# Attention in one written order of single operations, small matmuls between single dense matmuls

## The chip, the cores and the metric

The kernel runs on 1 core of one Trainium2 chip. The metric is device time in microseconds (us), the median of 3 runs. Inside the core five engines work at once, each on a queue of its own that it takes strictly in the order in which the program was compiled: TensorE (PE, matmuls; the loading of a matmul's stationary operand is shown apart, as PEld), VectorE (DVE), ScalarE (ACT), GpSimd (POOL) and SyncE (SP, which here issues DMAs). Instructions wait for each other over semaphores.

## The reference

A pre-norm block over 2048 tokens of width 1024: attention with a compressive memory, then a channel MLP. What matters here, cut down:

```
D, H, Dh, N, L = 1024, 32, 32, 4, 512          # four segments of 512 tokens
y = layernorm(x);  q, k, v = y @ wq, y @ wk, y @ wv          # per head: 512 x 32 a segment
for s in range(N):
    p = softmax(q_s k_s^T * Dh**-0.5 + causal mask)          # 512 x 512
    a_dot = p @ v_s
    a_mem = (phi(q_s) @ M) / (phi(q_s) @ z + 1e-6)           # phi(t) = t+1 if t > 0 else exp(t)
    out_s = g * a_mem + (1 - g) * a_dot                      # g = sigmoid(beta), per head
    M += phi(k_s)^T @ v_s;  z += sum(phi(k_s))
h = x + concat(out) @ wo
h2 = h + (gelu(layernorm(layernorm(h)) @ w1 + b1) @ w2 + b2)
```

## The kernel before, in words

All products are done in a reduced fp32 form on pairs: a number is split into a high and a low part (`kh`, `kl`), and one product takes three matmuls (high by high, high by low, low by high), all added up in one PSUM tile.

The program does two halves of 1024 tokens, each with two segments: segments 0 and 1 in the first half, 2 and 3 in the second. In a half, attention goes through 8 groups `g` of four heads and two segments `sl`, so through 16 units. A unit has two sides that run at the same time, the second one unit late:

- **The dense side** (`dense`): three projections of the unit's group, `kps`, `qps`, `vps`, each 8 chunks of 3 matmuls of 128x512, so 72 single dense matmuls. From each projection follow copies and splits on ACT and DVE (`kh`, `kl`, `qh`, `ql`, `vt`), the feature maps (`e`, `r` and their sum), and 12 DMAs on SP that stack the parts of `k` into the tiles `ks`, and 12 for `qs`.
- **The heads of the unit before** (`heads`, `slot`): for each of four heads, the scores `pqk` (4 matmuls of 128 to 512 columns, function `qk`), the negated scaled maximum on DVE (`mx`), the exponential on ACT, the normalising on POOL (`norm`), 10 transposes of 128x128 into `ppt` (`ptr`), their high part on ACT (`pth`) and low part on DVE (`ptl`), and 8 matmuls into `po` (`av`), then the output on ACT and DVE (`ot`). A head is spread over three slots: scores in one, transposes in the next, `po` in the one after.
- **Small matmuls** of 128 columns: 4 transposes each of `pk` (into `pkn`), `vt` (into `vn`) and `om` (into `pom`), 12 matmuls into `pm` (reading the memory, segments 1 to 3) and 12 into `pmm` (its update, segments 0 to 2). A unit has up to 36 of these, a unit of segment 3 has 20, one of segment 0 has 20. `pm` is read by four DVE operations (`memory`), `pmm` by five (`update`: four adds into `MZ` and one more).

PSUM has three buffers (tag `d`) for all of the projections, `pkn`, `vn`, `pm`, `pmm` and `pom`, two for `pqk`, two for `ppt`, one for `po`.

What sets the order around the change: `PLAN` is six steps a slot, and one step is taken after each chunk of three dense matmuls; `one_small` puts a small matmul ahead of a transpose or between two `po` matmuls; `late` holds the second part of a unit's small work. In the attention part the program's order is then a proposal: the framework's scheduler may place an instruction earlier or later on its engine by its own planned times. Only where the code uses `in_order` (the opening, the parts after attention) is the written order binding. The last unit's heads run beside the first matmuls of the output projection (`wo_first`, tiles `pwo`), and during the last dense unit seven loads `orr` bring outputs back from DRAM, which ACT copies into `oh` and DVE or POOL splits (`load_o`).

Of the kernel before, what the change touches and what calls it, by code (L numbers as in the profile page):

```python
# [9 lines left out]
F32 = mybir.dt.float32  # L10
# [6 lines left out]
P = 128  # L17
# [11 lines left out]
RA, RH, RS, PD, PS = 1.3, 14, 0.7, 20, 3  # L29
PLAN = ('q1 S2', 'q0 n0 a0', 'q2 t0 a1', 'q3 n2 s0 o', 't1', 's1 t2')  # L30
# [12 lines left out]
def build(tc, x, wq, wk, wv, wo, beta, w1, b1, w2, b2, out):  # L43
# [292 lines left out]
    def attention(half, first):  # L336
# [15 lines left out]
        def phi_parts(ps):  # L352
            e, r = tmp("e"), tmp("r")
            nc.scalar.activation(e, ps, AF.Exp)
            nc.scalar.activation(r, ps, AF.Relu)
            return e, r

        def phi_sum(parts, name, acc=None):
            o = tmp(name)
            nc.vector.scalar_tensor_tensor(o, parts[0], 1.0, parts[1], op0=ALU.min, op1=ALU.add, accum_out=acc)  # L360
            return o

        def stack(a, b, name, order):
            out = []
            for j in range(4):
                st = ab.tile([96, 512], F32R, tag=name, name=name, bufs=5)
                for blk, src in enumerate(order):
                    nc.sync.dma_start(raw(st[32 * blk:32 * blk + 32, :]), raw((a, b)[src][32 * j:32 * j + 32, :]))
                out.append(st)
            return out  # L370

        small = []

        def one_small():
            if small:
                small.pop(0)()

        def smalls(name, groups, last):
# [12 lines left out]
            small.extend(partial(one, k, n) for k in range(len(groups)) for n in range(3))  # L391

        def dense(g, sl, ws, u):
            s = 2 * half + sl
            behind = acts.pop("late", iter(()))
            kps = ws.pop("kps", None)
            if kps is None:
                kps = ps_dense("kps")
                for c in project(ws["k"], sl, "kps", kps):
                    if c >= 2:  # L400
                        next(behind, None)
                    yield
            kh, kl = tmpr("kh"), tmpr("kl")
            nc.scalar.copy(kh, kps)
            if s < 3:
                kparts = phi_parts(kps)
            qps = ps_dense("qps")
            for c in project(ws["q"], sl, "qps", qps):
                if c == 0:
                    nc.vector.tensor_tensor(kl, kps, raw(kh), op=ALU.subtract)  # L410
                    u["ks"] = stack(kh, kl, "ks", (0, 1, 0))
                if c == 2 and s < 3:
                    zc = ab.tile([P, 64], F32, name="zc", bufs=2)[:, 0:1]
                    pk = phi_sum(kparts, "pk", zc)
                next(behind, None)
                yield
            qh, ql = tmpr("qh"), tmpr("ql")
            nc.scalar.copy(qh, qps)
            if s > 0:
                qparts = phi_parts(qps)  # L420

            vps = ps_dense("vps")
            for c in project(ws["v"], sl, "vps", vps):
                if c == 0:
                    nc.vector.tensor_tensor(ql, qps, raw(qh), op=ALU.subtract)
                    u["qs"] = stack(qh, ql, "qs", (0, 0, 1))
                if s > 0:
                    if c == 2:
                        pq = phi_sum(qparts, "pq")
                    if c == 4:  # L430
                        while small:
                            one_small()
                        pqh, pql = tmpr("pqh"), tmpr("pql")
                        mzh = ab.tile([P, 256], F32R, name="mzh", bufs=1)[:, 0:132]
                        mzl = ab.tile([P, 256], F32R, name="mzl", bufs=1)[:, 0:132]
                        nc.scalar.copy(pqh, pq)
                        nc.vector.tensor_copy(mzh, MZ[:, g, :])
                        nc.gpsimd.tensor_tensor(mzl, MZ[:, g, :], raw(mzh), op=ALU.subtract)
                    if c == 5:
                        nc.gpsimd.tensor_tensor(pql, pq, raw(pqh), op=ALU.subtract)  # L440
                if c == 1 and s < 3:
                    pkn = ps_dense("pkn")
                    for i in range(4):
                        nc.tensor.transpose(pkn[:, i * P:(i + 1) * P], pk[:, i * P:(i + 1) * P], ident)
                    pkh, pkl = tmpr("pkh"), tmpr("pkl")
                    nc.scalar.copy(pkh, pkn)
                if c == 2 and s < 3:
                    nc.vector.tensor_tensor(pkl, pkn, raw(pkh), op=ALU.subtract)
                next(behind, None)
                yield  # L450
# [6 lines left out]
            def late():  # L457
# [39 lines left out]
                while len(small) > total - left:  # L497
                    yield
# [899 lines left out]
```

## Time and profile before

| what | value |
|---|---|
| median of 3 runs | 2358.24 us (2356.2 to 2359.72) |
| span of the profiled execution, first to last instruction | 2354.0 us |
| TensorE clock granted, mean | 0.995 |
| PE, share of the span | 97% |
| DVE, ACT, POOL, share of the span | 67%, 52%, 45% |

Of the profiled execution the profile gives the span alone; the runs are 2.2 to 5.7 us above it.

The units with heads are the stretches from 72 to 485 us (first half) and from 968 to 1377 us (second half). In them PE is busy 97% to 99% of the time, DVE about 76%, ACT about 71%.

How to read the rows: a timeline row gives the start, the duration, the engine, the line, the operation and `out<-in`. Matmuls are pipelined and their ends are modelled, so a dense matmul is shown with 0.39 us although the next one starts 0.23 us after it. What a matmul costs PE is therefore the distance from its start to the next start, and idle time in front of a matmul can hide behind the shown duration of the one ahead.

### The profile page before, as it was taken

To read this page: it belongs to the slowest core of one execution; us is meant where nothing else is said; L and a number is where in the kernel's file an instruction comes from. 1 tells how busy PE (TensorE), PEld (TensorE's weight loads), DVE (VectorE), ACT (ScalarE), POOL (GpSimd) and SP (SyncE) were. 2 spreads that over 40 slices of the span, in tenths; PEclk is the share of its full clock that TensorE was granted. 3 is DMA by queue.
4 is the path that set the end of the run, shared out by engine and by line. 5 is a ranking of instruction groups with operands and counts; after the bars stand their busy time and mean duration, and the time that the engine had idled before them with its cause. 6 is when DMAs were issued, how large, how long until landed. Compare 5 with 4: busy or idle time off the path is not lost.

```text
span 2354.0 us, 35355 instructions
## 1 busy us (share of the span) xinstructions
PE 2288.6 (97%) x11769; PEld 1893.4 (80%) x11769; DVE 1575.9 (67%) x3334; ACT 1228.8 (52%) x2557; POOL 1058.4 (45%) x1037
## 2 busy tenths in 40 slices
PE   7999999999999999999999999999999999999999
PEld 6888888878878887888888877778887888888887
DVE  6777777776655565777777777564566676566753
ACT  5676776785453444777777776363343233222321
POOL 4444444445243442555555545252444564255430
PEclk9999999999999999999999999999999999999999
DMA  5333333345365654433333334466557976576762
GB/s 172 95 89 91 86 81 87 83 115 174 127 196 171 192 161 137 124 83 84 88 83 85 89 93 132 152 198 175 168 176 251 341 254 204 160 251 222 255 219 94
DMA packets 322719, 355.36 MB, mean 151 GB/s; under 512 B 26190, under 2 KB 218730, under 8 KB 322538
## 3 DMA queue, kind: packets, MB, share of 16 engines
q1 hardware_dynamic: 259370, 316.40, 44.7%
q10 hardware_dynamic: 63168, 36.71, 5.2%
q8 instruction: 93, 1.52, 0.3%
q14 instruction: 88, 0.72, 0.1%
HBM read 226.59 MB, written 76.09 MB: 129 GB/s over the span
## 4 chain that ended last, share of the span: by engine, by line
PE 73%; DVE 9%; ACT 7%; DMA 4%; POOL 3%; issue 3%; SPq 1%; ACTq 0%; POOLq 0%; DVEq 0%
PE po L1235 21%; PE bps L856 8%; PE dps L856 5%; PE ppt L555 5%; PE po L575 4%; PE cps L856 4%; PE pqk L523 3%; PE kps L114 2%; PE kps L115 2%; PE kps L116 2%; PE vps L114 2%; PE vps L115 2%; PE vps L116 2%; PE qps L114 2%; PE qps L115 2%
## 5 line engine op out<-in xcount | busy, mean ns | idle before, releaser
L539 POOL TENSOR_SCALAR pr<-pr,nm,gate 128x128 f32<-128x128 f32 (+3 forms) x512 | 320.9, 636 | 400.6 <-DVE nm L536 293.1
L532 ACT ACTIVATE pr<-pr,mx 128x256 f32<-128x256 f32 (+3 forms) x512 | 287.6, 562 | 179.1 <-DVE mx L524 176.5
L524 DVE CUSTOM_DVE_ANT_0 pr<-pqk,mask 128x256 f32<-128x256 f32 (+3 forms) x512 | 243.5, 484 | 37.7 <-PE pqk L523 35.2
L562 DVE TENSOR_TENSOR ptl<-ppt,pth 128x512 fp32r<-128x512 f32 (+1 forms) x384 | 227.2, 597 | 59.5 <-ACT pth L557 57.4
L555 PE MATMUL ppt<-ident,pr 128*128 128x128 f32 x1280 | 223.2, 277 | 1.8 <-DVE ptl L562 1.8
L557 ACT CAST pth<-ppt 128x512 fp32r<-128x512 f32 (+1 forms) x384 | 194.0, 518 | 42.3 <-PE ppt L555 36.7
L1245 DVE TENSOR_TENSOR c<-c,po 128x512 f32<-128x512 f32 x160 | 105.3, 683 | 146.1 <-PE po L1235 146.1
L555 PEld LDWEIGHTS ppt<-ident,pr 128*128 128x128 f32 x1280 | 164.4, 140 | 32.1 <-DVE ptl L562 3.6
L91 POOL TENSOR_TENSOR wl<-wr,wh 128x1024 fp32r<-128x1024 f32 x53 | 126.8, 2392 | 90.8 <-DVE wh L88 31.0
L523 PE MATMUL pqk<-ks,qs 96*128 96x256 f32 (+3 forms) x512 | 163.3, 320 | 1.6 <-DVE mx L524 1.6
L575 PE MATMUL po<-ptl,vs 128*64 128x512 f32 (+3 forms) x512 | 154.8, 312 | 5.9 <-DVE ptl L562 5.7
L575 PE MATMUL po<-pth,vs 128*64 128x512 f32 (+3 forms) x512 | 156.3, 327 | 2.2 <-ACT pth L557 2.1
L1235 PE MATMUL po<-w2h,zh 128*128 128x512 f32 x378 | 120.8, 389 | 0.0
L523 PEld LDWEIGHTS pqk<-ks,qs 96*128 96x128 f32 x512 | 96.6, 189 | 27.1 <-DVE mx L524 7.0
L536 DVE RECIPROCAL nm<-mx 128x2 f32<-128x2 f32 x256 | 42.2, 165 | 109.0 <-ACT pr L532 108.7
L968 POOL TENSOR_TENSOR s<-r 128x512 f32<-128x512 f32 x28 | 43.1, 1540 | 158.9 <-DVE sa L984 117.6
L1105 POOL TENSOR_TENSOR w2r<-w2r 128x512 f32<-128x512 f32 x54 | 85.4, 1593 | 62.3 <-DMA w2r<-in_B_w 62.3
L856 PE MATMUL bps<-zh,sa 128*128 128x512 f32 x336 | 110.7, 390 | 1.6 <-DVE u L998 1.6
L856 PE MATMUL bps<-zh,sb 128*128 128x512 f32 x336 | 111.0, 391 | 0.9 <-DVE u L1010 0.9
L114 PE MATMUL kps<-yh,wh 128*128 128x512 f32 (+1 forms) x264 | 110.2, 417 | 0.6 <-ACT yh L144 0.6
L114 PE MATMUL vps<-yh,wh 128*128 128x512 f32 x256 | 109.0, 426 | 0.2 <-ACT omt L505 0.2
L114 PE MATMUL qps<-yh,wh 128*128 128x512 f32 x256 | 106.8, 417 | 0.0
(237 smaller groups left out, 6748.0 us busy)
## 6 DMA issues: line engine op xcount, KB each, us to landing
hr<-h_dram SPq DMA_DIRECT2D x112, 448.0 KB, 4.8
w2r<-in_B_w SPq DMA_DIRECT2D x122, 256.0 KB, 4.4
r<-in_B_w SPq DMA_DIRECT2D x56, 512.0 KB, 4.6
h_dram<-ht ACTq DMA_DIRECT2D x84, 256.0 KB, 3.8
ks<-kh SPq DMA_DIRECT2D x256, 64.0 KB, 2.0
qs<-qh SPq DMA_DIRECT2D x256, 64.0 KB, 2.0
wr<-in_A_wo SPq DMA_DIRECT2D x32, 512.0 KB, 4.0
wx<-in_B_w SPq DMA_DIRECT2D x56, 256.0 KB, 3.7
```

Of the source, the lines that this page charges most:

```text
L114: nc.tensor.matmul(ps, ah, bh, start=first, stop=False)
L115: nc.tensor.matmul(ps, ah, bl, start=False, stop=False)
L523: nc.tensor.matmul(pqk[:, :n], u["qs"][j][:, i * P:(i + 1) * P], u["ks"][j][:, 0:n], start=True, stop=True)
L524: nc.vector.tensor_tensor_reduce(out=st["pr"][:, offs[i]:offs[i] + n], in0=pqk[:, :n], in1=mask[:, 512 - n:512], op0=ALU.add, op1=ALU.min, ...
L532: nc.scalar.activation(pi, pi, AF.Exp, bias=mx[:, i:i + 1], scale=-1.0, accum_out=mx[:, 4 + i:5 + i])
L539: nc.gpsimd.tensor_scalar(pi, pi, nm[:, 4 + k:5 + k], gate[:, 1, 4 * g + j:4 * g + j + 1], op0=ALU.mult, op1=ALU.mult)
L555: nc.tensor.transpose(ppt[:, o:o + P], pr[:, offs[i] + jk * P:offs[i] + (jk + 1) * P], ident)
L557: nc.scalar.copy(pth[:, base:base + w], ppt[:, :w])
L562: nc.vector.tensor_tensor(o, x0, x1, op=ALU.subtract)
L575: nc.tensor.matmul(po[:, P * jk:], v, st[part][:, koff[jk]:koff[jk] + w], start=(jk, part) == (0, "pth"), stop=(jk, part) == (2, "ptl"))
L856: nc.tensor.matmul(ps, x_[:, c, :], y_[:, c, :], start=first and c == 0 and n == 0, stop=last and c == 3 and n == 2, skip_group_check=True)
L1235: nc.tensor.matmul(ps, x_[:, k], y_[k], start=opens and k == 0 and i == 0, stop=closes and k == self.KP - 1 and i == 2, skip_group_check=True)
```

## The change

The attention part is written as single operations at single places. A step is now one dense matmul (`D` in `PLAN`), 18 a slot, and between two `D` stand the operations of the heads one by one: `q` a score matmul, `x` its maximum, `e` the exponential, `r` the reciprocal, `n` the normalising, `t` one transpose, `c` and `s` the high and the low part, `a` one `po` matmul (`h` high, `l` low), `v` and `o` the output. `m` takes the next small matmul from the list `line`. The copies, splits and DMAs that follow a projection, and the loads and splits of the next group's weights, stand at numbered places of a clock that ticks once a dense matmul (`AT`); what follows a small product is issued when a given number of further small matmuls has been taken (`AFTER`). In the attention part this order is then binding on PE, DVE, ACT and POOL (`in_order(*ATT)`), and in the first output projection on PE (`in_order(*END)`), which is stepped by single matmuls as well. SP is not bound. The tiles `pth` and `ptl` are split in three with one, two and one buffers in place of two for the whole. The `ks` stacking is issued at place 37 of the 72 and `qs` at 56; before they stood behind the first chunk of the next projection. The arithmetic is the same: in two units next to each other PE issues the same 376 matmuls of the same shapes.

```diff
-RA, RH, RS, PD, PS = 1.3, 14, 0.7, 20, 3
-PLAN = ('q1 S2', 'q0 n0 a0', 'q2 t0 a1', 'q3 n2 s0 o', 't1', 's1 t2')
+RA, RH, RS, PD, PS = 1.3, 42, 0.7, 20, 3
+ATT = (E_.PE, E_.DVE, E_.Activation, E_.Pool)
+END = (E_.PE,)
+PLAN = ('q1 m D x1 e1 q0 x0 D e0 m ah0 m ah1 S2 m r0 n1 D al0 n0 t00 D t01 q2 x2 t02 D t03 c0 al3 '
...
+AT = dict(kh=24, ke=27, kr=27, kl=25, ks=37, pk=30, qh=48, qe=52, qr=55, ql=50, qs=56, pq=66, vt=72, lk=70, hk=96, ok=98, lq=91, hq=125, oq=127, lv=122, hv=146, ov=146)
+AFTER = dict(pkh=0, pkl=2, vh=0, vl=2, mem=0, upd=0, omt=0)
...
-        def project(w, sl, name, ps):
-            yh, yl = acts["y", sl]
-            for c in range(DC):
-                mm3(ps, w[0][:, c, :], w[1][:, c, :], yh[:, c, :], yl[:, c, :], c == 0, c == DC - 1)
-                yield c
...
+        def tick():
+            clock[0] += 1
+            for op in due.pop(clock[0], ()):
+                op()
...
+        def small():
+            while line:
+                matmul, op = line.pop(0)
+                op()
+                if matmul:
+                    return
...
+                for c in range(DC):
+                    for n, (a, b) in enumerate(((w[0], yh), (w[0], yl), (w[1], yh))):
+                        nc.tensor.matmul(ps, a[:, c, :], b[:, c, :], start=c == 0 and n == 0, stop=c == DC - 1 and n == 2)
+                        tick()
+                        if (c, n) != (DC - 1, 2):
+                            yield
...
+            vps = yield from product("v")
+            vt = tmp("vt")
+            at(position("vt"), lambda: nc.scalar.copy(vt, vps))
...
+            turned(vt, "vn", values)
...
+                               for c in range(4)], lambda pmm: then(AFTER["upd"], partial(update, pmm)))
+            if s > 0:
+                turned(om, "pom", lambda pom: then(AFTER["omt"], lambda: nc.scalar.copy(omt, pom)))
...
+            for op in PLAN:
+                if op == "D":
+                    yield
+                elif op == "m":
+                    small()
+                else:
+                    st, fn = ops[op[0]]
+                    if st:
+                        fn(st, *[int(c) if c.isdigit() else c for c in op[1:]])
...
-                        d = hooked(d, lambda k: load_o(half, 0, k, ab), 3, NG - 1)
+                        d = hooked(d, lambda k: load_o(half, 0, k, ab), 9, NG - 1)
...
-        rest = attention(half, first)
+        with in_order(*ATT):
+            rest = attention(half, first)
+        acts.pop("last")
```

Three places show what moves. In the rows, `kps`, `qps`, `vps` with 128x512 are dense matmuls, `pm` and `pmm` small ones, `ppt`, `vn` and `pom` transposes, and `64x512` is a `po` matmul with 64 columns of weights.

First, PE in the middle of a unit of the first half; before:

```order
L523 MATMUL pqk<-ks,qs 128x384
L386 MATMUL pm<-mzl,pqh 128x132
L555 MATMUL ppt<-ident,pr 128x128
L386 MATMUL pm<-mzh,pql 128x132
L555 MATMUL ppt<-ident,pr 128x128
L386 MATMUL pmm<-vs,pkh 128x128
L555 MATMUL ppt<-ident,pr 128x128
L386 MATMUL pmm<-vs,pkh 128x128
L555 MATMUL ppt<-ident,pr 128x128
L386 MATMUL pmm<-vs,pkl 128x128
L575 MATMUL po<-pth,vs 64x128
```

The same stretch of the order now:

```order
L447 MATMUL qps<-yl_191,wh 128x512
L400 MATMUL pmm<-vs,pkh 128x128
L447 MATMUL qps<-yh_190,wl 128x512
L564 MATMUL pqk<-ks,qs 128x256
L400 MATMUL pmm<-vs,pkh 128x128
L447 MATMUL qps<-yh_190,wh 128x512
L564 MATMUL pqk<-ks,qs 128x128
L447 MATMUL qps<-yl_191,wh 128x512
L400 MATMUL pmm<-vs,pkl 128x128
L611 MATMUL po<-pth_1099,vs 64x512
L400 MATMUL pmm<-vs,pkh 128x128
L611 MATMUL po<-pth_1136,vs 64x384
```

Short matmuls that stood in a row between triples of dense ones now stand alone, many of them directly ahead of a dense matmul.

Second, PE in the second half, at the end of the small work of segment 2; before:

```order
L116 MATMUL qps<-yh_10254,wl 128x512
L386 MATMUL pmm<-vs,pkl 128x128
L504 MATMUL pom<-ident,om 128x128
L386 MATMUL pmm<-vs,pkh 128x128
L504 MATMUL pom<-ident,om 128x128
```

Now the last `pmm` and the first `pom` stand one dense matmul apart:

```order
L447 MATMUL vps<-yl_10511,wh 128x512
L400 MATMUL pmm<-vs,pkh 128x128
L595 MATMUL ppt<-ident,pr 128x128
L447 MATMUL vps<-yh_10510,wl 128x512
L595 MATMUL ppt<-ident,pr 128x128
L400 MATMUL pmm<-vs,pkl 128x128
L447 MATMUL vps<-yh_10510,wh 128x512
L386 MATMUL pom<-ident,om 128x128
```

There the built program puts `pom` into the PSUM buffer that `pmm` had, so the first `pom` waits for DVE's reads of `pmm`; in the first half, and before, it has another buffer. What DVE now has in its queue at that place:

```order
L568 ISA pr,mx<-pqk,mask 128x512
L568 ISA mx 128x1
L624 TENSOR_TENSOR ot<-po,ot 32x512
L459 TENSOR_TENSOR ql<-qps,qh 128x512
L578 RECIPROCAL nm<-mx 128x2
L542 TENSOR_TENSOR MZ<-pmm,MZ 32x32 x4
L543 SCALAR_TENSOR_TENSOR MZ<-hsel,zc,MZ 128x4
```

The five operations on `MZ` stand behind a reciprocal that itself needs ACT's exponential. The next unit begins, in the same half, with `vn` right behind the last dense matmul of `vps`, because segment 3 has no `pkn` ahead of it:

```order
L447 MATMUL vps<-yl_10511,wh 128x512
L447 MATMUL vps<-yh_10510,wl 128x512
L595 MATMUL ppt<-ident,pr 128x128
L386 MATMUL vn<-ident,vt 128x128 x2
L447 MATMUL kps<-yh_9564,wh 128x512
```

`vn` reads `vt`, which ACT copies from the finished `vps`.

Third, ACT in the last dense unit of the first half; before:

```order
L90 CAST wh<-wr 128x1024
L418 CAST qh<-qps 128x512
L666 CAST oh_6474<-orr 128x512
L580 COPY ot<-po 32x512
L532 ACTIVATE pr,mx<-pr,mx 128x512
L666 CAST oh_6474<-orr 128x512
L354 ACTIVATE e<-qps 128x512
```

and now:

```order
L421 ACTIVATE e<-qps 128x512
L97 CAST wh<-wr 128x1024
L720 CAST oh_6717<-orr 128x512
L421 ACTIVATE r<-qps 128x512
L599 CAST pth_6966<-ppt 128x256
L575 ACTIVATE pr,mx<-pr,mx 128x256
```

The copy into `oh` now has a place fixed between `e` and `r`, and the load that it waits for can be issued only when its buffer is freed, which here is by an operation on ACT just ahead.

More of the change, by code (lines that the diff above doesn't have):

```diff
@@ L407, in dense @@
[L407 to L417, printed above, removed]
@@ L418, in dense @@
-            nc.scalar.copy(qh, qps)
-            if s > 0:
[L420 to L450, printed above, removed]
@@ L1279, in pre @@
                     yield
-        interleave(wo_first(half, hts, pre()), rest, RA, RH, RS)
+        with in_order(*END):
+            interleave(wo_first(half, hts, pre()), rest, RA, RH, RS)
+        acts.pop("last")
         if half == 0:
```

383 lines of the change are left out of this document (213 added, 170 removed).

## The prediction

> **What bounds the kernel now.** I read the page's busy times first, then the busy time by stretches, then PE's waits, and last the start times of single matmuls.
>
> ```profile
> PE 2288.6 (97%) x11769; PEld 1893.4 (80%) x11769; DVE 1575.9 (67%) x3334; ACT 1228.8 (52%) x2557; POOL 1058.4 (45%) x1037
> ```
>
> ```profile
> 72.20:484.90 412.70, 402.11 (x2443) 337.86 (x2442) 308.69 (x955) 288.46 (x737) 192.42 (x245) 1.00 0.33 84
> 968.30:1377.00 408.70, 403.48 (x2439) 337.70 (x2438) 316.61 (x967) 294.70 (x748) 214.14 (x266) 1.00 0.34 85
> ...
> 1377.00:1425.00 48.00, 43.10 (x260) 35.41 (x259) 37.27 (x104) 37.27 (x88) 26.36 (x31) 1.00 0.42 121
> ```
>
> PE is the bound. In the two long stretches of the attention units (columns: length, then PE, PEld, DVE, ACT, POOL busy, clock, DMA) PE stands idle 10.6 and 5.2 us; only there, and at their ends, can a new order save anything. What PE waits for there:
>
> ```profile
> PE pmm L386 <- DVE kl L410: 5.9, 7, 0.8
> PE po L575 <- DVE ptl L562: 3.7, 5, 0.7
> ```
>
> ```profile
> PE pom L504 <- DVE om L474: 2.6, 7, 0.5
> PE pqk L523 <- DVE mx L524: 1.4, 7, 0.2
> ```
>
> Each is a DVE operation that came late, once in two units. Part of a wait hides behind the drawn length of the matmul ahead, so I also measure two units from one first `kps` to the next but one, in the first half and in the second:
>
> ```profile
> 326.81 0.48 PE L114 MATMUL kps<-yh,wh 128*128 128x512 f32 x1
> ...
> 390.63 0.48 PE L114 MATMUL kps<-yh,wh 128*128 128x512 f32 x1
> ```
>
> ```profile
> 1157.12 0.48 PE L114 MATMUL kps<-yh,wh 128*128 128x512 f32 x1
> ...
> 1220.06 0.48 PE L114 MATMUL kps<-yh,wh 128*128 128x512 f32 x1
> ```
>
> A pair takes 63.82 us and 62.94 us. Against this stands what its 376 matmuls cost without waits. The prices are distances between starts:
>
> ```profile
> 304.54 0.39 PE L115 MATMUL kps<-yl,wh 128*128 128x512 f32 x1
> 304.76 0.39 PE L116 MATMUL kps<-yh,wl 128*128 128x512 f32 x1
> 304.99 0.22 PE L523 MATMUL pqk<-ks,qs 96*128 96x128 f32 x1
> 305.05 0.28 PE L386 MATMUL pmm<-vs,pkh 128*128 128x128 f32 x1
> 305.16 0.40 PE L575 MATMUL po<-pth,vs 128*64 128x512 f32 x1
> 305.40 0.22 PE L386 MATMUL pmm<-vs,pkh 128*128 128x128 f32 x1
> 305.46 0.39 PE L575 MATMUL po<-ptl,vs 128*64 128x512 f32 x1
> 305.69 0.22 PE L386 MATMUL pmm<-vs,pkl 128*128 128x128 f32 x1
> 305.75 0.34 PE L575 MATMUL po<-pth,vs 128*64 128x384 f32 x1
> 305.92 0.22 PE L386 MATMUL pmm<-vs,pkh 128*128 128x128 f32 x1
> 305.98 0.34 PE L575 MATMUL po<-ptl,vs 128*64 128x384 f32 x1
> 306.16 0.40 PE L114 MATMUL qps<-yh,wh 128*128 128x512 f32 x1
> ```
>
> ```profile
> 325.30 0.39 PE L116 MATMUL vps<-yh,wl 128*128 128x512 f32 x1
> 325.53 0.60 PE L555 MATMUL ppt<-ident,pr 128*128 128x128 f32 x4
> 325.89 0.48 PE L114 MATMUL vps<-yh,wh 128*128 128x512 f32 x1
> 326.20 0.40 PE L115 MATMUL vps<-yl,wh 128*128 128x512 f32 x1
> ```
>
> 512 columns cost 0.23 us (a dense matmul 0.22 to 0.235, I take 0.2315), 384 cost 0.175, and a small one between two `po` costs 0.06. By the same scale 256 columns are 0.12. Four transposes and a dense one last 0.67 us from 325.53 to 326.20, which leaves 0.11 for a transpose. A pair is then 144 dense x 0.2315 = 33.3; 100 transposes x 0.11 = 11.0; 8 heads' scores x (0.23 + 0.175 + 0.12 + 0.06) = 4.7; 16 such sets for `po` = 9.4; 36 small x 0.06 = 2.2; and 0.5 for small ones between transposes (below). Sum 61.1 us. So waits take 2.7 us of a pair in the first half and 1.8 in the second.
>
> **What the change removes.** All of those waits, if every distance now suffices: the stretches hold 6.5 pairs each, 6.5 x (2.7 + 1.8) = 29 us. The lower bound is the idle time seen, 10.6 + 5.2 = 16 us. I take -29, since the four waits named are what the new places pull apart: a low part stands a good eight matmuls ahead of its `po`.
>
> **What it adds on PE: the loading of weights behind a short matmul.** The same 376 matmuls have other neighbours. A lone short matmul directly ahead of a dense one exists once as a clean row in the trace of before:
>
> ```profile
> 941.66 0.39 PE L116 MATMUL kps<-yh,wl 128*128 128x512 f32 x1
> 941.89 0.22 PE L523 MATMUL pqk<-ks,qs 96*128 96x128 f32 x1
> 941.95 0.45 PE L114 MATMUL kps<-yh,wh 128*128 128x512 f32 x1
> 942.24 0.40 PE L115 MATMUL kps<-yl,wh 128*128 128x512 f32 x1
> ```
>
> From the short one to the dense one behind next are 0.35 us; less 0.23 for the dense one, the short one costs 0.12, where a matmul of as many columns ahead of one with 64 columns of weights costs 0.06 (305.69 to 305.75). The opening says the same: there matmuls of 256 columns with 128 columns of weights follow each other every 0.12 us:
>
> ```profile
> 20.05 0.28 PE L116 MATMUL kps<-yh,wl 128*128 128x256 f32 x1
> 20.18 0.28 PE L114 MATMUL kps<-yh,wh 128*128 128x256 f32 x1
> ```
>
> So about 0.12 us must pass between the start of a matmul and that of the next one with 128 columns of weights; 0.22 or a transpose's 0.11 covers it, 0.06 does not. In the new order a pair has 35 short ones ahead of a dense matmul (8 `pqk` and 8 `po` of 128 columns, 19 small), in the old none. That is 35 x 0.06 = 2.1 us. Against it, small ones next to transposes become rare:
>
> ```profile
> 301.67 0.22 PE L386 MATMUL pmm<-vs,pkh 128*128 128x128 f32 x1
> ...
> 302.66 0.39 PE L115 MATMUL kps<-yl,wh 128*128 128x512 f32 x1
> ```
>
> Here four small ones, four transposes and a dense one took 0.99 us; less 0.23 and 0.44 each small one costs 0.08 instead of 0.06. Of 25 such places 20 go: -0.4. Three short ones ahead of small ones go too: -0.2. Net 1.5 us a pair, and with 8 pairs of heads in each half +24 us. Bounds: 0, if the load finds other cover, and 35, if a lone transpose costs 0.12 as well (68 a pair stand ahead of a dense matmul, before 16).
>
> The Trainium skill, "TensorE: Matmul & The Clock Gate", section "LDWEIGHTS (loading the stationary operand)", puts a load at its columns over 1.2, in ns: 107 ns for 128 columns. The rows above show 0.12 us. By 107 the 24 us would be some 17.
>
> **What it adds in waits.** In the second half the first `pom` waits until DVE has read the last `pmm` (its PSUM buffer), and `vn` stands right behind `vps`:
>
> ```profile
> L489 DVE TENSOR_TENSOR MZ<-pmm,MZ x24: 157/186/197, 308.6 to 472.8; 32x32 f32<-32x32 f32 x24
> L490 DVE SCALAR_TENSOR_TENSOR MZ<-hsel,zc,MZ x6: 223/790/1361, 312.4 to 468.5; 128x4 f32<-128x4 f32 x6
> ```
>
> ```profile
> 487.11 0.60 ACT L452 COPY vt<-vps 128x512 f32<-128x512 f32 x1
> ```
>
> The last `pmm` shows its result about 0.3 us after its start (drawn 0.22 to 0.31), four additions of 0.186 and one of at least 0.22 make 0.97, in all 1.3 with the hand-over; the order has 0.12 + 0.23 in between. So 1.0 us at least, up to 1.5 where the reciprocal ahead on DVE still waits for ACT's exponential; I take 1.2, 8 times. `vn`: the last dense matmul is done 0.4 us after its start, the copy takes 0.6, and 0.23 + 0.11 lie between: 0.7, 8 times. Together 15 us, between 5 (DVE and ACT far ahead) and 25 (both late by one more operation). While PE waits, what is queued behind `pom` on PE is the dense chain itself, so it counts in full. In the first half neither place exists; for late operations there I add 3 us (0 to 10), since DVE has a good quarter of its time left.
>
> At the ends of the halves ACT must now copy the returned outputs at fixed places, and some loads start just ahead of their copy:
>
> ```profile
> DMA to landing us min/median/max: 2.7/3.8/6.8
> ```
>
> If PE has about 1.3 us in hand, such a copy holds up ACT's high parts and with them PE by 2.5 us. Two a half look bare (the fifth and seventh): 4 x 2.5 = +10. The waits already there (the row from 1377 us shows 4.9 us of idle PE) shrink by half, -4. Net +6, between -6 and +15. The later `ks` and `qs` stacking costs nothing: 12 issues at under 0.6 us and 2 us of landing fit the 16 dense matmuls, some 7 us, before the next unit, and only the first head's tiles are needed then.
>
> **The sum.** -29 + 24 + 15 + 3 + 6 = +19 us on the span of 2354.0. The runs lie 2 to 6 us above the span and move alike, so 2358.24 + 19 = 2377 us.
>
> **Rivals.**
> 1. *Loads hidden: faster.* If lone short matmuls cost 0.06, PE would gain: the 24 us fall away, and the 0.6 a pair of old exposure goes as well (-10): -29 - 10 + 15 + 3 + 6 = -15, 2343 us. For it: loads do run beside a matmul, dense ones follow each other by 0.23. Against: 941.89, and the opening. It decides as soon as a short one costs under 0.08. The Trainium skill speaks for it: the same page, section "Architectural detail: the array is 16× 32×32, not 1× 128×128", says that PE's queue can pull weight loads ahead of running matmuls; the lone row shows no more than one load ahead.
> 2. *The new waits don't come:* DVE and ACT are ready, the loads early; -29 + 24 + 0 to 5 = -5 to 0, about 2355 us. For it: the quarter of free time on both. Against: `pom` needs five operations after `pmm` whatever DVE does.
> 3. *Fixed queues stall everywhere:* each operation now waits at the head of its queue. If each of the 128 heads loses 0.3 us more, +38: 2415 us. Against: most distances in the order are over 1.5 us.
>
> That the change does not do what it says is excluded: the built order shows it.
>
> **Chances.** Forecast (2362 to 2395) 0.57, rival 1 0.14, rival 2 0.16, rival 3 0.13. The range leaves out the far half of rivals 1 and 3: 2347 to 2402 us. A difference of 0.2%, 4.7 us, is about what can be told from none. Faster by more: rival 1 and a part of rival 2, 0.21; within: most of rival 2, 0.12; slower: 0.67.
>
> **What would show it.** In the profile after: a lone `pqk` of 128 columns to the dense matmul after next 0.35 us (0.29 for rival 1); PE waiting for `kl`, `ptl` in the first half gone; `pom` <- DVE `MZ` and `vn` <- ACT `vt` some 8 times each in the second half; ACT idle ahead of `oh`; a pair of about 63 us in the first half and 65 in the second. I would be wrong if pairs take 62 us in both halves, or if PE waits once a head.

## The result, and the profile after

The changed kernel takes 2414.56 us (median of 4 runs, 2410.04 to 2419.6) beside 2357.22 us for the kernel before on the same chip: a ratio of 1.0237, 95% interval 1.0215 to 1.0259. It is 57 us slower; forecast were 19 us, in a range up to 2402 us. Spans below are those of the profiled executions, 2408.0 and 2354.0 us.

The page's first part of the changed kernel, which answers to the first row of the prediction:

```profile
PE 2317.8 (96%) x11769; PEld 1887.1 (78%) x11769; DVE 1589.3 (66%) x3334; ACT 1228.2 (51%) x2557; POOL 1070.3 (44%) x1037
```

The share says almost nothing. The time is found by cutting both spans at the same matmuls: the first `kps` with 512 columns (which opens the first unit with heads), the second unit, the last unit, the first `cps` behind the output projection, and the same again in the second half. Busy time by stretches of the kernel before (columns: length, then PE, PEld, DVE, ACT, POOL busy, granted clock, DMA share, GB/s):

```profile
0.00:42.26 42.26, 28.54 (x165) 23.10 (x165) 26.96 (x60) 23.62 (x38) 18.41 (x38) 1.00 0.66 189
42.26:72.17 29.91, 28.54 (x154) 23.70 (x155) 20.16 (x60) 18.50 (x50) 15.02 (x18) 0.94 0.52 153
72.17:486.82 414.65, 404.06 (x2455) 339.44 (x2454) 310.42 (x959) 290.20 (x741) 192.42 (x245) 1.00 0.33 84
486.82:634.38 147.56, 142.53 (x745) 116.30 (x744) 99.53 (x213) 84.03 (x165) 67.15 (x75) 1.00 0.44 143
...
910.94:939.35 28.41, 26.24 (x129) 20.61 (x127) 15.53 (x31) 17.97 (x26) 11.98 (x19) 1.00 0.52 145
939.35:968.31 28.96, 28.73 (x170) 24.08 (x171) 21.66 (x71) 19.32 (x51) 15.14 (x18) 1.00 0.54 156
968.31:1377.68 409.37, 404.14 (x2443) 338.20 (x2442) 317.09 (x968) 295.35 (x750) 214.14 (x266) 1.00 0.34 85
1377.68:1529.21 151.53, 143.64 (x745) 117.36 (x744) 101.28 (x213) 82.91 (x163) 65.33 (x76) 0.99 0.42 135
```

and of the kernel after:

```profile
0.00:53.43 53.43, 32.52 (x162) 26.21 (x162) 27.40 (x52) 22.40 (x31) 18.53 (x38) 0.90 0.63 189
53.43:81.88 28.45, 28.01 (x158) 22.33 (x157) 20.54 (x66) 20.13 (x56) 13.65 (x16) 1.00 0.34 88
81.88:497.62 415.74, 411.58 (x2455) 333.44 (x2453) 314.70 (x960) 289.18 (x742) 196.07 (x248) 1.00 0.33 84
497.62:663.09 165.47, 149.46 (x747) 119.10 (x746) 101.85 (x215) 84.22 (x165) 66.25 (x75) 0.96 0.39 126
...
939.42:980.99 41.57, 32.13 (x130) 24.69 (x129) 16.45 (x29) 17.98 (x24) 10.66 (x17) 0.84 0.46 131
980.99:1012.11 31.12, 29.70 (x173) 23.89 (x172) 23.92 (x73) 20.06 (x54) 15.88 (x19) 1.00 0.45 119
1012.11:1430.16 418.05, 409.79 (x2438) 331.67 (x2438) 315.39 (x966) 293.51 (x747) 215.31 (x266) 1.00 0.32 82
1430.16:1584.94 154.78, 145.12 (x748) 117.02 (x747) 102.70 (x216) 83.61 (x164) 69.78 (x78) 0.98 0.41 132
```

Length after less length before, row by row:

| stretch | change, us |
|---|---|
| opening and first dense unit, first half | +11.2 |
| first unit with heads | -1.5 |
| thirteen units | +1.1 |
| last dense unit and output projection | +17.9 |
| first dense unit, second half | +13.2 |
| first unit with heads | +2.2 |
| thirteen units | +8.7 |
| last dense unit and output projection | +3.2 |
| the two long stretches left out above | -2.0 |
| sum | +54.0 |

The units with heads, on which nearly the whole prediction was spent, give 10.5 us. The starts of the halves give 24 and their ends 21. What PE waits for now (waits of the kernel after, whole span):

```profile
PE pt L149 <- DVE yl L153: 13.6, 8, 3.8
PE ppt L595 <- DVE ptl L603: 9.3, 5, 2.5
...
PE pom L386 <- DVE MZ L542: 8.0, 8, 2.2
PE vn L386 <- ACT vt L484: 7.5, 9, 2.5
...
PE pt L149 <- ACT xt L170: 7.2, 2, 3.9
...
PE pmm L400 <- DVE vs L510: 4.9, 7, 0.7
```

`pom` and `vn` are there as forecast: in the second half `pom` waits 7 times (7.1 us) and `vn` 8 times (6.6 us); the rest of these two rows stands at the end of the first half. The second row, `ptl`, stands at the ends of the halves. The first and the fifth row shown were not forecast: L149 are the transposes of the LayerNorm of the *next segment* (`ln1`), which runs beside the first dense unit of each half, where there are no heads yet. Its rows in the opening, PE first, then ACT:

```profile
24.11 0.39 PE L447 MATMUL qps<-yh,wl 128*128 128x512 f32 x1
27.83 0.66 PE L149 MATMUL pt<-ident,xt 128*128 128x128 f32 x4 [3.33 <-ACT xt L170]
28.24 0.48 PE L447 MATMUL qps<-yh,wh 128*128 128x512 f32 x1
...
29.02 0.46 PE L447 MATMUL qps<-yh,wh 128*128 128x512 f32 x1
31.85 1.12 PE L149 MATMUL pt<-ident,xt 128*128 128x128 f32 x4 [2.37 <-DVE yl L153]
```

```profile
26.53 1.24 ACT L170 ACTIVATE xt<-xt,nb,v 128x1024 f32<-128x1024 f32 x1 [1.55 <-POOL nb L141]
29.36 1.24 ACT L170 ACTIVATE xt<-xt,nb,v 128x1024 f32<-128x1024 f32 x1 [1.58 <-POOL nb L141]
30.50 0.57 ACT L151 CAST yh<-pt 128x512 fp32r<-128x512 f32 x1
```

The transposes stand at a fixed place among the `qps` matmuls. The first set comes four dense matmuls ahead of the second, which needs the same PSUM buffer, and that is read by `yh` on ACT and `yl` on DVE. On ACT `yh` stands behind the next tile's `xt`, which waits for POOL. So PE, with some forty dense matmuls of the unit queued behind the transpose, stands still 2 to 4 us at a time. In the kernel before there were nine dense matmuls between the same two sets (transposes at 24.66 and 28.44 us), and the second set waited 1.0 us for `yl`.

One row of the end of the first half, the row on ACT that the prediction priced:

```profile
ACT oh L720 <- DMA orr<-o_dram: 8.1, 3, 4.2
```

These are three waits, 8.1 us together; in the second half there are two, 5.5 us together. And the clock: the rows above show 0.90 and 0.84 at the starts of the halves, and at the end of the first it is down to half for some microseconds behind waits of PE of about 2 us or more. One such stretch:

```profile
522.00:528.00 6.00, 5.99 (x22) 4.59 (x23) 3.60 (x13) 3.55 (x10) 2.47 (x4) 0.54 0.47 143
```

### The profile page after: what moved, and what is told of

The parts are those of the page before. It is cut to its first block, busy times and chain, and to the rows that moved or that the text cites. A ratio compares the mean times of both kernels' runs of the same rounds, so it can differ in the third digit from the quotient of the medians.

```text
span 2408.0 us, 35642 instructions
## 1 busy us (share of the span) xinstructions
PE 2317.8 (96%) x11769; PEld 1887.1 (78%) x11769; DVE 1589.3 (66%) x3334; ACT 1228.2 (51%) x2557; POOL 1070.3 (44%) x1037
## 4 chain that ended last, share of the span: by engine, by line
PE 78%; DVE 6%; ACT 5%; DMA 4%; POOL 3%; issue 3%; SPq 0%; ACTq 0%; POOLq 0%; DVEq 0%
PE po L1294 19%; PE bps L915 8%; PE kps L447 7%; PE qps L447 7%; PE vps L447 6%; PE po L611 6%; PE dps L915 5%; PE ppt L595 5%; PE pwo L754 4%; PE cps L915 4%; PE pqk L564 3%; PE pm L400 1%; PE pmm L400 1%; DMA c<-h_dram 1%; DVE sa L1043 1%
## 5 line engine op out<-in xcount | busy, mean ns | idle before, releaser
L583 POOL TENSOR_SCALAR pr<-pr,nm,gate 128x256 f32<-128x256 f32 (+3 forms) x512 | 327.0, 648 | 491.2 <-DVE nm L578 369.1
L595 PE MATMUL ppt<-ident,pr 128*128 128x128 f32 x1280 | 348.3, 273 | 10.6 <-DVE ptl L603 9.3
L595 PEld LDWEIGHTS ppt<-ident,pr 128*128 128x128 f32 x1280 | 180.2, 141 | 44.3 <-POOL pr L583 5.5
L611 PE MATMUL po<-ptl,vs 128*64 128x512 f32 (+3 forms) x512 | 173.5, 339 | 0.0
L611 PE MATMUL po<-pth,vs 128*64 128x512 f32 (+3 forms) x512 | 125.2, 318 | 1.9 <-DVE ot L624 1.6
L671 POOL TENSOR_TENSOR wl<-wr,wh 128x1024 fp32r<-128x1024 f32 x45 | 107.9, 2397 | 24.7 <-DVE wh L668 19.7
L447 PE MATMUL qps<-yl,wh 128*128 128x512 f32 x256 | 117.1, 457 | 0.0
L447 PE MATMUL vps<-yl,wh 128*128 128x512 f32 x256 | 116.1, 454 | 0.0
L447 PE MATMUL vps<-yh,wl 128*128 128x512 f32 x256 | 116.1, 453 | 0.0
L447 PE MATMUL kps<-yh,wl 128*128 128x512 f32 x248 | 114.8, 463 | 0.1
```

Of the source, the lines that this page charges most:

```text
L447: nc.tensor.matmul(ps, a[:, c, :], b[:, c, :], start=c == 0 and n == 0, stop=c == DC - 1 and n == 2)
L583: nc.gpsimd.tensor_scalar(pi, pi, nm[:, 4 + k:5 + k], gate[:, 1, 4 * g + j:4 * g + j + 1], op0=ALU.mult, op1=ALU.mult)
L595: nc.tensor.transpose(st["ppt", n][:, i * P:(i + 1) * P], st["pr"][:, offs[q] + jk * P:offs[q] + (jk + 1) * P], ident)
L611: nc.tensor.matmul(po[:, P * jk:], u["vs"][:, 4 * jk + j, :], st[part, n][:, o:o + 512 - P * jk], start=(part, jk) == ("h", 0), stop=(part ...
L671: nc.gpsimd.tensor_tensor(ws[n][1], raws[n], raw(ws[n][0]), op=ALU.subtract)
```

## The experiments

All ratios are to the kernel before, run on the same chip beside each kernel; the changed kernel has 1.0237. Expectations are quoted as they were put down beforehand.

**1. The first unit outside the binding order.**

```diff
-        with in_order(*ATT):
-            rest = attention(half, first)
+        rest = attention(half, first)
...
+        order = ExitStack()
...
+                if prev is None:                      # behind the first dense unit
+                    order.enter_context(in_order(*ATT))
                 prev = u
             ws = after
+        order.close()
```

> The binding order starts only behind the first dense unit of each half, so the transposes of the next segment's LayerNorm (`pt` <- `xt`), with their copies and the opening's constants, may be moved by the scheduler again, as in the kernel before. Everything else is as in the changed kernel. Theory A (the binding of the LayerNorm steps costs the time at the starts of the halves: in the changed kernel the first `kps` of a unit with heads comes 11.2 us later, and the first unit of the second half is 13.1 us longer, where PE waits 20.8 us for `yl` and `xt`): both go, 2414.6 - 24 = 2390 us (2384 to 2396), the first such `kps` at 42 to 44 us, the waits of L149's transposes under 8 us. Rival B (every operation at the head of a fixed queue costs a little, wherever it stands; the starts only show what comes late first, such as weights or loads): the time moves on into the next units, 2408 to 2415 us.

Measured: 2392.89 us, ratio 1.0141 (1.0124 to 1.0158), 23 us less. The two stretches that lost are back:

```profile
0.00:42.75 42.75, 28.26 (x158) 23.02 (x158) 25.45 (x52) 22.59 (x34) 18.62 (x38) 1.00 0.63 184
930.10:958.68 28.58, 25.84 (x126) 20.28 (x124) 14.61 (x28) 17.54 (x24) 10.26 (x17) 1.00 0.53 147
```

Theory A holds: the binding of the first dense unit cost the starts. PE's waits at the `pt` of `ln1` fall from 20.8 us to 4.9, and the granted clock there is 1.00 again. Some 3 us come back in the two units that follow (30.5 and 32.0 us long for 28.5 and 31.1), nothing in the thirteen units (415.3 us) or at the end of the half (165.0). The run freed the whole first dense unit; that it was the steps of `ln1` in it is read from these waits.

**2. The `oh` copies outside the binding order.**

```diff
-            if engines and ins.engine not in engines:
+            if engines and ins.engine not in engines or ins.name in acts["free"]:
...
+        acts["free"] |= {op.ins.name, low.ins.name}        # in load_o: the copy to oh and the low part ol
```

> The fourteen copies of returned outputs into `oh` and their low parts `ol` are taken out of the binding order, everything else stays as in the changed kernel. Theory A (in the last dense unit of the first half ACT stands 8.1 us at `oh` waiting for the loads `orr`, and `ot`, `pth` and with them PE stand behind it; the PE clock then drops as well): the end of the first half, from the last unit's first `kps` to the first `cps`, falls from 165.5 us to about 152, the second half's by 1 to 3: 2400 us (2395 to 2405). Rival B (the end is long because the last heads have too little dense work to stand between, whatever ACT does): 2411 to 2415 us, with the same PE idle in front of `ppt` and `po`.

Measured: 2406.01 us, 1.0198 (1.0181 to 1.0215), 9 us less. The two ends:

```profile
498.27:657.89 159.62, 147.57 (x747) 117.21 (x746) 100.14 (x215) 84.00 (x165) 63.82 (x75) 0.98 0.40 131
1425.52:1574.44 148.92, 142.28 (x748) 115.19 (x747) 102.03 (x216) 83.32 (x164) 70.34 (x78) 1.00 0.43 137
```

Each end gains 5.9 us, and ACT's wait for `orr` at the first falls from 8.1 to 0.6 us. The mechanism is there, but in the first half it is only a third of the 17.9 us (the end is 159.6 us where theory A had 152), and the second half, which lost 3.2 us, is now shorter than before the change. The time lies between the two theories.

**3. Both releases.** The edits of 1 and 2 together.

> Both releases at once: the first unit of each half and the copies into `oh` are outside the binding order. Theory A: the two gains add up, 2414.6 - 24 - 14 = 2376 us (2370 to 2383), which leaves the steady units of the second half (about +9 us) and some rest at the ends as what the change costs. Rival B: 2405 to 2415 us.

Measured: 2383.66 us, 1.0099 (1.0084 to 1.0114). The gains add up (23 + 9), to 32 of the 57 us; the time is just above theory A's range.

**4. Nothing bound.** Both `in_order` of the attention part and of the first output projection taken away; the written places stay as a proposal to the scheduler.

> The same written places, but nothing in the attention part and the first output projection is bound: the scheduler may move every operation, as in the kernel before. Theory A (the losses come from binding at the starts and ends, the places themselves cost about nothing in the first half's steady units and 1.6 us a pair in the second): the starts and ends come back to those of the kernel before, and the `pom` and `vn` waits of the second half shrink too: 2360 us (2352 to 2372). Rival B (the placing itself costs, by the lone short matmuls ahead of dense ones, and only the binding keeps the units free of waits): units of 64.5 us or more in both halves, 2375 to 2390 us.

Measured: 2378.86 us, 1.0080 (1.0063 to 1.0096), the figure of rival B. The starts are back and the ends nearly, as theory A has it (the end of the first half is 151.2 us, for 147.6 in the kernel before), but the thirteen units of the first half grow to 421.1 us, and those of the second stay at 418.0:

```profile
PE ppt L595 <- POOL pr L583: 5.3, 12, 0.7
PE pom L386 <- DVE ql L459: 2.7, 7, 0.4
```

These first-half waits aren't there when the units are bound, which is what B said of the binding. So binding is worth something in the steady units and costs at their two ends.

**5. Empty places ahead of three products** (on top of 3).

```diff
+            if s == 3:
+                line.extend([(True, lambda: None)] * 3)
             turned(vt, "vn", values)
...
+            if s == 0:
+                line.extend([(True, lambda: None)] * 2)    # ahead of pmm
...
+            if s == 2:
+                line.extend([(True, lambda: None)] * 3)
             if s > 0:
                 turned(om, "pom", ...)
```

> The kernel with both releases (first unit and `oh` copies outside the order), and empty places in the list of small matmuls: three ahead of `pom` in segment 2, three ahead of `vn` in segment 3, two ahead of `pmm` in segment 0. The work is the same, those products only come two to three small places later. Theory A (term of the new waits: in the second half PE waits 8.0 us for DVE's `MZ` and 7.5 us for ACT's `vt`, in the first 4.9 us for DVE's `vs`, because too little stands in between): the waits shrink to a third, second-half pairs go from 64.5 to about 63.2 us, first-half ones from 63.9 to 63.4: 2383.7 - 9 - 3 = 2372 us (2367 to 2376). Rival B (DVE and ACT are late by their own queues, the wait moves along with the product): 2380 to 2387 us, the same waits by name.

Measured: 2385.16 us, 1.0110 (1.0095 to 1.0125), no gain in all, because the halves part:

```profile
71.78:481.21 409.43, 409.43 (x2456) 333.38 (x2454) 314.81 (x960) 289.04 (x742) 196.04 (x248) 1.00 0.33 85
974.89:1398.33 423.44, 409.37 (x2441) 331.92 (x2439) 322.16 (x968) 295.03 (x750) 215.36 (x266) 1.00 0.32 82
```

```profile
PE pom L386 <- DVE om L530: 14.1, 7, 2.0
```

In the first half theory A is right and more than right: PE is busy for the whole 409.43 us, and the profile shows no wait (6 us less). In the second the waits for `MZ` and `vt` are gone and another has come, once a pair. In segment 3 no `pmm` stands between `pm` and `pom`, and the third `pom` reads the part of `om` that DVE makes from the last `pm`. In experiment 3 DVE begins with that 0.3 us after the last `pm` (1187.77 and 1188.03 us). Here the last `pm` starts at 1182.61 us, at a place where other operations stand ahead in DVE's fixed order, and DVE begins 3.1 us later:

```profile
1185.76 0.17 DVE L527 TENSOR_SCALAR rg<-pm 128x8 f32<-128x8 f32 x1
```

```profile
1187.61 0.33 PE L386 MATMUL pom<-ident,om 128*128 128x128 f32 x1 [2.01 <-DVE om L530]
```

So in this half rival B is nearer: the new place is early for DVE's own queue. Experiment 9 gives that `pom` five places of its own.

**6. The two short matmuls of each head ahead of `po`** (on top of 3).

```diff
-PLAN = ('q1 m D x1 e1 q0 x0 D e0 m ah0 m ah1 S2 m r0 n1 D al0 n0 t00 D t01 q2 x2 t02 D t03 c0 al3 '
-        'D m al1 ah3 e2 s0 ...
+PLAN = ('q1 m D x1 e1 D q0 x0 ah0 e0 m ah1 S2 m r0 n1 D m al0 n0 t00 D t01 q2 x2 t02 D t03 c0 '
+        'D m al3 al1 ah3 e2 s0 ...
```

> The kernel with both releases, and in `PLAN` three entries a slot moved, so that the two short matmuls that each head had directly ahead of a dense one stand ahead of a `po` matmul with 64 columns of weights: `q0` (128 columns) goes behind the next dense matmul, ahead of `ah0`; `al3` goes ahead of `al1`; one small matmul goes from ahead of `ah0` to ahead of `al0`. No matmul is added or left out. Theory A (the weight-load term: a short matmul directly ahead of a dense one costs 0.12 us in place of 0.06): 2 x 0.06 x 128 heads = 15 us less, 2383.7 - 15 = 2369 us (2365 to 2373), pairs shorter by 0.9 us in both halves. Rival B (the load of weights is hidden there, or the pairs are set by waits): 2381 to 2387 us.

Measured: 2378.92 us, 1.0085 (1.0070 to 1.0100), 3 us less than experiment 3, where 15 were expected. The price is nearly right. In the changed kernel the lone `pqk`, from its start to the dense matmul after next (here a transpose follows the dense one), then the same `pqk` ahead of a `po` of 512 columns:

```profile
306.64 0.22 PE L564 MATMUL pqk<-ks,qs 96*128 96x128 f32 x1
306.70 0.45 PE L447 MATMUL kps<-yh,wl 128*128 128x512 f32 x1
306.99 0.27 PE L386 MATMUL pkn<-ident,ph 128*128 128x128 f32 x1
```

```profile
207.76 0.22 PE L562 MATMUL pqk<-ks,qs 96*128 96x128 f32 x1
207.82 0.40 PE L609 MATMUL po<-pth,vs 128*64 128x512 f32 x1
208.06 0.22 PE L398 MATMUL pm<-mzh,pqh 128*128 128x132 f32 x1
```

0.35 us and 0.30 us. The thirteen units of the first half fall by 4.1 us (415.5 to 411.4), where 0.9 a pair would have been 6. In the second half they gain nothing (419.2 for 418.1): `qps` now waits for DVE's `om`, 0.6 us seven times. The term exists, by 0.05 us a matmul in these rows; over the 104 moved matmuls of the first half's thirteen units 4.1 us are 0.04.

**7. The last unit and the output projection unbound too** (the `oh` copies with them).

```diff
+                if (g, sl) == (NG - 1, 0):
+                    order.close()
...
-        with in_order(*END):
-            interleave(wo_first(half, hts, pre()), rest, RA, RH, RS)
-        acts.pop("last")
+        interleave(wo_first(half, hts, pre()), rest, RA, RH, RS)
```

> The binding order holds only from the second unit of each half to the one before its last; the last dense unit and the first output projection with the last heads are left to the scheduler, as in the kernel before (with nothing bound at all, the end of the first half took 151.2 us, with the `oh` copies alone released 159.3). Theory A (what is left at the first half's end, a DVE `ot` and `om` that PE waits 2.5 and 3.2 us for, comes from the fixed order there): the end falls to 150 to 152 us: 2383.7 - 8 = 2376 us (2371 to 2379). Rival B (it comes from the places in the list, with too little dense work between the last heads): 2381 to 2386 us.

Measured: 2375.37 us, 1.0073 (1.0058 to 1.0088). The end of the first half is 153.0 us, for 159.3 with only the copies released there (experiment 3) and 165.5 with all bound. So of its 17.9 us, 6.2 are the copies and 6.3 the fixed order of the rest; 5.5 stay. PE's wait for `om` there falls from 3.2 us to 0.7, and that of 2.5 us for `ot` is gone. In the second half part of it is lost again: the end takes 151.4 us, for 148.6 in experiment 3.

**8. No short matmul directly ahead of a dense one**, with free ends.

```diff
+PLAN = ('q1 D x1 e1 D q0 x0 ah0 e0 m ah1 S2 r0 n1 D m al0 n0 t00 D t01 q2 x2 t02 D t03 c0 '
+        'D m al3 al1 m ah3 e2 s0 ah2 m al2 q3 D x3 m t10 v D D m t11 D o m t12 D m t13 e3 r2 n2 D m t20 c1 '
+        'n3 D D m t21 D D c2 s1 D D D').split()
```

> The order bound only in the steady units (as in the run with free ends), and `PLAN` written so that no short matmul stands directly ahead of a dense one: `q0`, `al3` and five small ones stand ahead of `po` matmuls, the other small ones ahead of a transpose. Same matmuls, eleven places for small ones a slot as before. Theory A: by the prices of the prediction's rows a pair costs 61.0 us without waits, in place of 62.9, so 16 pairs save about 29 us, the free ends 8, and the new places happen to stretch the `pom` and `vn` distances (5 to 10 us less of waiting): 2383.7 - 42 = 2342 us (2333 to 2352), faster than the kernel before. Rival B (units are set by ACT's and DVE's late operations as soon as PE's own cost falls): 2360 to 2375 us, with PE waiting for `ptl`, `pth` or `mx` once a head.

Measured: 2407.7 us, 1.0205 (1.0188 to 1.0222), 32 us slower than experiment 7. PE's busy time in the thirteen units fell (408.5 and 405.1 us, for 411.3 and 410.1 in experiment 7), but the units became longer (429.1 and 434.0 us, for 415.5 and 418.5). Waits took more than the gain; in the first half:

```profile
PE pm L398 <- DVE om L526: 11.5, 7, 1.7
PE pm L398 <- DVE pkl L491: 3.1, 7, 0.5
```

In the second half the largest are those of `pom` for ACT's `r` (9.2 us) and DVE's `MZ` (8.0). The small products now stand closer together, which leaves DVE and ACT less time between two of them; that this is the cause was not tested. They aren't the waits once a head of rival B (`ptl`, `pth`, `mx`): these stay away. Neither theory had a loss of this size.

**9. Steady units bound, ends free, distances right, two short ones covered.** Experiments 5, 6 and 7 together, with five empty places ahead of `pom` in segment 3.

> The order bound only in the steady units, the two short matmuls a head ahead of `po` (as in the run with covered short ones), and empty places in the list: two ahead of `pmm` in segment 0, three ahead of `vn` in segment 3, three ahead of `pom` in segment 2 and five in segment 3, where the spaced run had put `pom` right behind the last `pm`. Theory A (a steady unit costs the sum of its matmuls' prices as soon as these waits have their distance: the spaced run's first half had no wait left and 62.87 us a pair): 62.1 us a pair in both halves, so the thirteen units from the second on take 405 us in each, against 414.7 and 409.4 in the kernel before: with the ends some 5 us longer than there, 2347 us (2341 to 2353), faster than the kernel before. Rival B (waits only change their name, as `pom` did in the spaced run): second-half pairs of 64 us or more, 2358 to 2370 us.

Measured: 2341.17 us, 0.9921 (0.9904 to 0.9938): 0.8% faster than the kernel before, and 3% faster than the changed one.

```profile
71.49:476.27 404.78, 404.78 (x2456) 331.75 (x2454) 330.82 (x962) 288.86 (x742) 196.28 (x248) 1.00 0.34 86
...
964.70:1368.31 403.61, 403.61 (x2441) 331.31 (x2439) 323.62 (x970) 294.24 (x750) 216.12 (x267) 1.00 0.34 86
```

In both long stretches the busy time of PE equals the length. The profile shows no wait there any more (pauses shorter than the drawn length of a matmul would not show). A pair takes 62.3 and 62.1 us; as far as the profile shows, what is left to gain there is the matmuls' prices themselves.

**10. Three more small ones ahead of a transpose.** As 9, with `m` moved ahead of `t00`, `t20` and `t21`.

> As the ninth run, and three more small places a slot moved by at most one dense matmul, so that they stand directly ahead of a transpose in place of a dense matmul (`m` ahead of `t00`, `t20` and `t21`). Theory A: a small one ahead of a transpose costs 0.06 to 0.07 in place of 0.12, 61.4 us a pair in both halves, another 8 us less: 2339 us (2332 to 2346). Rival B: the small places move apart unevenly and a wait for `om`, `pkl` or `MZ` comes in, as with the packed list: 2350 us or more.

Measured: 2345.4 us, 0.9938 (0.9923 to 0.9952), not the 8 us less. The second half takes 402.6 us (1 us less), the first 408.2 (3 more), with small waits that experiment 9 has not:

```profile
PE pom L384 <- DVE ql L457: 2.2, 7, 0.3
PE pmm L398 <- DVE vs L508: 1.4, 6, 0.2
```

By its figure the time is at the upper edge of theory A's range, and the difference to experiment 9 is small against the intervals. But the 8 us did not come, and waits came in, as rival B has it: places moved by one dense matmul can be enough to lose a distance.

**11. Experiment 9's places, nothing bound.**

> The ninth run's places with nothing bound in the attention part: does the steady part gain by being bound at all? Theory A (yes: with nothing bound, at the changed kernel's places, the thirteen units of the first half took 421.1 us, 5 to 6 more than bound, since the scheduler moves operations by its own times and brings waits back): first-half stretch 411 us or more where the bound one has 405, in all 2355 us or more. Rival B (the binding is worth nothing, the places and distances do it all): within 4 us of the ninth run.

Measured: 2355.12 us, 0.9980 (0.9969 to 0.9992), 14 us more than experiment 9. The first half's thirteen units take 417.1 us for 404.8, the second half's 403.4 for 403.6. So with good places the binding is worth 12 us, all of it in the first half.

## Why the prediction was wrong, point by point

The direction was right, the size was not: +57 us for +19.

- **The step that failed: "PE stands idle 10.6 and 5.2 us; only there, and at their ends, can a new order save anything."** The sentence is true of what can be saved, and the sum was then written as if it also said where the order can *cost*. The opening and the first dense unit of each half have no term at all. They lie inside the binding order as well, with the steps of `ln1` in them; the two stretches became 11.2 and 13.2 us longer, and experiment 1 gave 23 us back. With +24 in the sum the forecast would have been 2401 us.
- **"Two a half look bare ... 4 x 2.5 = +10 ... Net +6"**: right in mechanism, mis-sized. ACT waits 8.1 and 5.5 us for `orr`, in three waits and two, where 10 in all were priced. But the ends became 21 us longer (17.9 + 3.2), not 6: the old waits did not shrink by half, they grew, since the binding of the other operations holds PE too (experiments 3 and 7: 6.2 us for the copies and 6.3 for the rest in the first half), and some of the waits of about 2 us or more are followed by matmuls at half clock (0.96 granted in that stretch, 1.00 before). At least 3.4 us of the first half's end came back in no run (it is shortest in experiment 11, 151.0 us) and stay unexplained.
- **"What the change removes" (-29)**: right in mechanism. The four waits named are gone from the steady units; in the first half only `pmm` <- `vs` is left, and experiments 5 and 9 show it with none at all. How many of the 29 us this gave was not measured apart from what the change adds.
- **"The loading of weights behind a short matmul" (+24)**: right in kind; the covered `pqk` is 0.05 us cheaper, where 0.06 was taken, so some 18 (35 x 0.05 less 0.6, for 16 pairs). Of the two rows that carried the 0.12, that of the opening says nothing: 256 columns cost 0.12 by the prediction's own scale, whatever the load. The 107 ns that follow for 128 columns, as an estimate, from the columns over 1.2 of the Trainium skill, "TensorE: Matmul & The Clock Gate", section "LDWEIGHTS (loading the stationary operand)", would make the difference 0.047, the 0.12 of the prediction 0.06; the measured 0.05 is nearer to the page.
- **"`pom` ... 8 times", "`vn` ... 8 times" (+15)**: 7.1 and 6.6 us in the second half, 13.7 together. In the steady units a wait is shorter than priced (0.8 us for 1.2, 0.6 for 0.7); 4.7 us are one long wait of each in the last dense unit.
- **"Late operations" of the first half (+3)**: `pmm` <- `vs`, 4.9 us, seven times 0.7.
- **The units as a whole**: -29 + 24 + 15 + 3 = +13 was forecast for them, +10.5 is measured (-1.5, +1.1, +2.2, +8.7). The two are not quite the same thing: the 24 and the 15 were added up over 8 pairs a half, and these stretches hold 7. A pair takes 64.0 us in the first half, for 63 forecast, and 64.5 in the second, for 65.
- **The later `ks` and `qs` stacking** costs nothing, as said: no matmul of the steady units waits for them.
- **Rival 1** (loads hidden) is out by the rows of experiment 6. **Rival 2** is out: the waits came. **Rival 3** named 2415 us and the time is 2414.6, but its mechanism, 0.3 us lost by each of 128 heads, isn't there: of the waits of the first half's thirteen units only `vs`, once a pair, is left. Fixed queues did stall, but at the starts and the ends. The figure is right by luck.

## What to carry to other kernels

Here a binding order was worth something only where the work is periodic (12 us in the steady units of the first half, none in those of the second, once the distances were set), and cost where something else runs beside it: the first and last rounds, with their loads, normalisations and returned tiles. So price a change of order at every stretch that it covers, not only at the long ones, and try binding the steady part alone; here that, with the distances of three products mended and two short matmuls a head moved, turned +2.4% into -0.8%. And a wait that is taken away by a distance must be looked for at the next product that needs the same engine: experiments 5, 8 and 10 each moved products and got waits of other names.

## What the hardware showed that was not expected

A wait of PE can cost more than its length. From the end of the first half in experiment 3, a chain of dense matmuls with nothing else between:

```profile
612.27 0.39 PE L759 MATMUL pwo<-wh,ol 128*128 128x512 f32 x1
614.30 0.59 PE L759 MATMUL pwo<-zh,oh 128*128 128x512 f32 x1 [1.64 <-DVE zl L153]
614.68 0.63 PE L759 MATMUL pwo<-zl,oh 128*128 128x512 f32 x1
...
617.67 0.54 PE L759 MATMUL pwo<-zh,ol 128*128 128x512 f32 x1
```

Behind a pause of 2.0 us from start to start, eight matmuls follow each other by 0.38 to 0.43 us, for 3.4 us, where they follow by 0.23 otherwise: 1.5 us more than the wait itself. In the changed kernel the stretch at 522 us (clock 0.54) shows the same, and the starts of the halves (0.90 and 0.84). Not every such pause does it: one of 2.2 us, at 542 us of the changed kernel, is followed by full clock. The traces record the granted clock, and it changes only on a grid of 3.41 us. In the 13 profiled executions, from 22 us on, every stretch of this grid at full clock in which PE was busy (as drawn) for less than 44% was followed by half clock, 65 of 65, and none with more than 62%; between them it went either way. The pause at 612.27 us leaves PE busy for 1.78 us of the stretch that ends at 614.56; the one at 542 us falls on both sides of an edge at 541.21, and the two stretches keep 2.48 and 2.54 us. The Trainium skill, "TensorE: Matmul & The Clock Gate", section "What's actually happening", has half the clock after an idle window of about 3.4 us that runs freely; the 3.4 us of half clock agree with that window, while the pause that set it off here was shorter than one: a window half idle was enough.
